# Linear attention and a Swish layer on one core: one batch's early steps a slot later, tangent products in their own chunk, a new order by hand

## The chip, the core and the metric

The kernel runs on one core of a Trainium2 chip. A core has a matrix engine (TensorE, PE in the profile; its weight loads are listed apart as PEld), a vector engine (VectorE, DVE), an engine for activations (ScalarE, ACT), a general engine (GpSimd, POOL) and a queue for transfers (SyncE, SP). The metric is the device time of one execution in microseconds, as the median of several runs.

## What is computed

The reference, cut to what matters. Eight batches of eight heads, 576 positions of 64 numbers; their attention output is the input of a two-layer block with 2048 columns in the middle.

```python
theta = pi / 2 * pos / S
phi(x) = concat(max(x, 0) * cos(theta), max(x, 0) * sin(theta))     # 64 -> 128
kv  = einsum('bhsf,bhsd->bhfd', phi(k), v)
z   = sum(phi(k), over s)
x   = einsum('bhsf,bhfd->bhsd', phi(q), kv) / (phi(q) . z + 1e-6)
# x as (8*576 tokens, 512)
h   = x @ w_in                          # 512 -> 2048
out = (h / (1 + exp(-beta * h))) @ w_out   # 2048 -> 512, float32
```

## The kernel before

The 4608 tokens are worked off in nine chunks of 512. A batch has 576 tokens, nine blocks of 64, so chunk c needs x of batches up to c; the attention of batch c+1 is worked between the matmuls of chunk c.

Attention of one batch: ReLU of q, k (`q_relu`, `k_relu`); v scaled by cosine and by sine (`v_scale`, on DVE or ACT); kv (`kv_mm`, copied out of PSUM by `kv_take`); the queries turned, on TensorE with an identity for batches 0 and 1 (`q_turn_pe`), by a transposing DMA after that (`q_turn_dma`). The cosine of the queries is divided out at the end, so that the second half of the features is the turned query times a table of tangents: the tangent product, `tan_mul`; `q_tan` runs it on GpSimd. `num_mm` multiplies by kv, `x_rden` and `x_mul` divide, and x is turned back (`x_turn_pe` or `x_turn_dma`) into the tile `xt` of its chunk.

The two layers: `h_plain` computes a block of 128 middle columns with four matmuls of 512 columns. `h_fast` does a 2x2 block scheme with seven products instead of eight for four pairs of column blocks (named X, Y, Z, V), and `o_fast` the same for the output of a chunk (x, y for its two halves). The operands of these products are sums and differences: `g_sum` for the middle activations, `x_sum` for x, `wh_sums` and `w_sums` for weights.

Every engine runs its instructions in the order in which the program gives them (`manual_schedule`). This order is written by hand. Three stretches matter here:

*Chunk 0's slots* (the loop at L783). Slots 0 to 15 compute middle columns; slots 16 to 23 multiply the first eight row blocks of `w_out` into the output; slots 24 to 31 one more row block each: slot 24 multiplies by block 8, slot 25 by block 9, up to block 15. Each slot is four matmuls of 512 columns. Before use a row block is cast and scaled by `cast_out(j)`, on DVE (L123) or, with "a", on ACT (L121). After the matmuls of a slot, the entry of the table `early` (L736) of that slot is run. `rest` (slot 4) gives DVE, in this order, casts 0 to 7, the scaling of v, and the ReLUs of k and q of batch 1. `second` is the turn of batch 1's queries with the casts from 8 on.

*Chunks 1 and 2*: a loop of 16 slots (middle columns), then the output products, with batches 2 and 3 between (`h_first` and the code after it). `att_q` does the ReLU and turn of the queries, `v_half` one scaling of v.

*Chunks 3 to 6*: `chunk` walks through the string `ORDER` (L874). p and sp are plain blocks and their activation; X1 to V7 products, and c1X, a2X, SaX and the like their copies, adds and activations; K and kt are kv and its copy; N0 the attention products, x0 to x2 the division and turn of a third of x, each into its own two PSUM banks; s01 to s34 the sums; g0, g1 the tangent products; ox1 to oy7 the output's products; k, q, v, w with a digit prepare the next batches; t the sums of x for the next chunk. When the operations of a set are done, `prep` calls the next load of k, q or v into the freed tile.

Of the kernel before, what the change touches and what calls it, by code (L numbers as in the profile page):

```python
# [17 lines left out]
NQ = 9  # L18
# [4 lines left out]
def kernel(  # L23
# [16 lines left out]
    B, H, S, D = q.shape  # L40
# [76 lines left out]
    def cast_out(j, eng="d"):  # L117
        i, jj = divmod(j, 4)
        st = stages["out", i]
        if eng == "a":  # L120
            nc.scalar.activation(wout[:, j, :], st[:, jj, :], AF.Copy, scale=rbeta[:, j : j + 1])  # L121
        else:
            nc.vector.tensor_scalar(wout[:, j, :], st[:, jj, :],  # L123
                                    scalar1=rbeta[:, j : j + 1], scalar2=None, op0=ALU.mult)
# [141 lines left out]
    def kv_mm(b, jp, bank, jjs=(0, 1)):  # L266
        t = kv_out(jp, bank)
        for n in range(NQ):
            for jj in jjs:
                for g in range(2):  # L270
                    hs = slice(g * HP, (g + 1) * HP)
                    nc.tensor.matmul(  # L272
                        t[jj * HP : (jj + 1) * HP, g], lhsT=rk[hs, n, 2 * jp + jj, :],
                        rhs=vb[hs, n, 2 * jp + jj].rearrange("q s e -> q (s e)"),
                        start=(n == 0), stop=(n == NQ - 1))
# [382 lines left out]
    got = x_rden(2, 0, 0, 7, (0,))  # L658
# [55 lines left out]
    def num_seven(jp, bank):  # L714
        for n in range(7):
            num_mm(1, n, jp, bank, n)
# [3 lines left out]
    def second():  # L720

        takes.append(q_turn_pe(1, 0, 4, hold=True))
        takes.append(q_turn_pe(1, 1, 6, hold=True))
        cast_out(8)
        takes[0]("act", 0)
        takes[0]("dve", 1)
        cast_out(9, "a")
        takes[0]("dve", 0)
        takes[0]("act", 1)
        cast_out(10)  # L730
        for e, i in (("act", 0), ("dve", 1), ("act", 1), ("dve", 0)):
            takes[1](e, i)
        for j in (11, 12, 14, 15):
            cast_out(j, "a")
# [1 line left out]
    early = {  # L736
        4: lambda: (num_mm(0, 8, 0, 2, 0), num_mm(0, 8, 1, 2, 1), rest()),
        15: lambda: v_scale(1, 1, eng="act"),
        22: lambda: (kv_mm(1, 0, 6), kv_mm(1, 1, 6), kv_take((0, 1), 6, "act")),
        23: second,  # L740
        25: lambda: (num_seven(0, 4), x_mul(x_rden(4, 0, 0, 7, (0,)), 0, 7), cast_out(13)),
        26: lambda: (num_seven(1, 6), x_mul(x_rden(6, 0, 0, 7, (1,)), 0, 7)),
        28: lambda: x_turn_pe(1, 0, 7, 4, ("act",), (0,)),
        29: lambda: x_turn_pe(1, 0, 7, 5, ("dve",), (1,)),
    }

    def num_rest():
# [23 lines left out]
        if b + 1 < B:  # L771
            load_raw(b + 1, "k")

    def kv_all(b, bank=6):
        kv_mm(b, 0, bank)
        kv_mm(b, 1, bank)
        kv_take((0, 1), bank)

    def x_part(b, t, bank):
        x_div(t, bank)  # L780
# [30 lines left out]
    for slot in range(16):  # L811
        h_group(1, slot)
        if slot == 0:
            num_rest()
            att_q(2)
            v_half(2, 0)
        if 3 <= slot < NQ:
            v_half(2, 1, slot, slot + 1, "act")
        if slot == 4:
            k_all(2)  # L820
            v_half(2, 1, 0, 3)
        elif slot == 6:
            w_sums()
        elif slot == 11:
            kv_all(2)
            for jp in range(2):
                tan_mul(nc.vector, qs_of(2)[:, jp], qts[0][:, jp], 0, NQ)
    q_relu(3, 0, "act")
# [28 lines left out]
    got = wh_sums(0)  # L857
# [9 lines left out]
    def k_piece(b, j):  # L867
# [4 lines left out]
            load_raw(b + 1, "k")  # L872

    ORDER = (  # L874
        "p0 Y1 X1 c1X p1 X5 c5X sp0 X6 X2 K c1Y X3 cuX kt Y6 X7 p2 a2X a3X Y5 sp1 a7X cuY c5Y Y7 Z1 SaX "
        "X4 c1Z p3 Y3 Y2 SbX sp2 a7Y Z2 s01 Y4 Z5 sp3 Z6 s03 a3Y a2Z p4 SbY V1 a2Y c5Z cuZ Z7 s02 a7Z p5 "
        "SaY c1V V6 Z3 s11 sp4 s12 cuV a3Z V2 Z4 s14 sp5 V5 SbZ c5V V7 p6 a2V V3 SaZ a7V a3V s21 sp6 SaV "
        "p7 s04 s13 V4 s22 SbV s23 sp7 s24 s31 s33 N0 k1 s32 ox1 c1o ox5 k3 c5o k2 ox6 s34 g0 g1 x0 k0 "
        "ox3 oy1 cuo c1y x2 o3x ox2 ox7 v8 oy5 x1 c5y o2x oy6 w8 q0 q1 cuy v2 v6 oy3 o7x v3 w1 oy7 w4 w3 "
        "w7 o7y ox4 v5 t3 w5 oy2 v4 c4x o3y v7 t1 w0 oy4 w6 t2 v1 c4y v0 o2y w2 t4")  # L880
    ORDER_LAST = (
        "E1 c1E E2 F1 X1 a2E c1X c1F X5 X2 E5 X6 c5X E6 cuX c5E cuE X3 a2X Y1 E3 X7 a3X c1Y a3E SaX a7X "
        "E7 SaE F6 Y5 F5 a7E X4 Y2 c5F Y6 SbX F2 F3 a2Y c5Y a2F cuF E4 Z1 Y3 cuY SbE c1Z a3F Y7 F7 a3Y "
# [40 lines left out]
    def chunk(c, b, x, y, parts):  # L924
        steady = {"X": (0, 2, 0, 1), "Y": (4, 3, 4, 5), "Z": (8, 0, 2, 1), "V": (12, 4, 3, 5)}
        end = {"X": (0, 6, 0, 1), "E": (2, 5, 3, 4), "Y": (4, 2, 0, 1), "F": (6, 7, 3, 4), "Z": (8, 6, 0, 1),
               "V": (12, 5, 3, 4)}
        pairs = {n: h_fast(c, at[0], at[1:]) for n, at in (steady if b < B else end).items()}

        def plain_bank(n):  # L930
            return (2 if n == 7 else 6 + n % 2) if b < B else (2, 7)[n % 2]

        plain = [2, 3, 6, 7, 10, 11, 14, 15]
        outs = {"x": x, "y": y}

        def q_next():
            if b + 3 < B:
                load_raw(b + 3, "q")

        def raw_next(name):  # L940
            if b + 2 < B:
                load_raw(b + 2, name)

        xs_all = {"x0", "x1", "x2"}
        take = prep(b, [
            ({"k0", "k1", "k2", "k3"} | xs_all, lambda: raw_next("k")),
            ({"q0", "q1"} | xs_all, q_next),
            ({f"{o}{n}" for o in "vw" for n in range(NQ)}, lambda: raw_next("v"))])
        last_sum = None
        for op in (ORDER if b < B else ORDER_END if c + 1 < NTC else ORDER_LAST).split():  # L950
            n = int(op[-1]) if op[-1].isdigit() else None
            if op == "K":
                kv_mm(b, 0, 4)
                kv_mm(b, 1, 4)
            elif op == "kt":
                kv_take((0, 1), 4)
            elif op[0] == "N":
                for t, bank in enumerate(parts):
                    num_all(b, t, bank)
            elif op[0] == "x":  # L960
                x_part(b, n, parts[n])
                take(op)
            elif op[0] in "kvwq":
                take(op)
            elif op[0] == "t":
                if c + 1 < NTC:
                    x_sum(c + 1, n)
            elif op[0] == "g":
                if b + 1 < B:
                    q_tan(b + 1, n, None if n else last_sum)  # L970
            elif op[0] == "p":
                h_plain(c, plain[n], plain_bank(n), 2 if n < SPLITS.get(c, (0, 0))[0] else 1)
            elif op[:2] == "sp":
                h_silu(c, plain[n], plain_bank(n))
            elif op[0] == "o" and n is not None:
                outs[op[1]][op[2]]()
            elif op[0] == "o":
                outs[op[2]]["a" + op[1]]()
            elif op[0] == "c" and op[2] in "xyo":
                outs["x" if op[2] == "o" else op[2]][op[:2]]()  # L980
            elif op[0] == "s":
                last_sum = g_sum(c, 2 * int(op[1]), 2 * int(op[1]) + 2, n)
            else:
                pair = op[0] if op[0] in pairs else op[-1]
                pairs[pair][op.replace(pair, "")]()
        if b + 2 < B:
            q_turn_dma(b + 2)

    def h_first(c):
        b = c + 1  # L990
        for slot in range(16):
            h_group(c, slot, 2 if slot < SPLITS.get(c, (0, 0))[0] else 1)
            if c == 2:
                if slot == 0:
                    k_all(b)
                    v_half(b, 1, 0, 4)
                if 1 <= slot < 6:
                    v_half(b, 1, slot + 3, slot + 4, "act")
                if slot == 3:
                    att_q(b + 1)  # L1000
                    wh_sums(4)
                if slot == 9:
                    wh_sums(8)
            if slot == (8 if c == 2 else 1):
                kv_all(b)
            if slot in (3, 7, 11):
                g_sums(c, slot // 2 - 1, slot // 2 + 1)
            elif slot in (13, 15):
                sums = g_sums(c, slot // 2, slot // 2 + 1)
        return sums  # L1010

    FAST = 3
    for c in range(2, NTC):
# [4 lines left out]
        if c >= FAST:  # L1018
            chunk(c, b, x, y, parts)
            continue  # L1020
        sums = h_first(c)
        for t, bank in enumerate(parts):
            num_all(b, t, bank)
        q_tan(b + 1, 0, sums)
        q_tan(b + 1, 1)
        for i, n in enumerate("156273"):
            x[n]()
            if n in "156":
# [15 lines left out]
        y["c5"]()  # L1044
        if c == FAST - 1:
            x_sums(c + 1)
            wh_sums(12)
        v_half(b + 1, 1, 2, 3, "act")
        y["6"]()
        y["cu"]()  # L1050
# [5 lines left out]
        y["3"]()  # L1056
        y["a3"]()
        v_half(b + 1, 0, 7, 9)
        v_half(b + 1, 1, 3, 9, "act")
        y["4"]()  # L1060
        y["c4"]()
# [31 lines left out]
```

## Time and profile before

| | |
|---|---|
| time, median of 3 | 278.01 us (277.81 to 278.37) |
| profiled execution, span on the core | 275.6 us |
| busy: PE, PEld, DVE, ACT, POOL | 268.9, 199.8, 221.0, 184.6, 67.8 us |
| granted TensorE clock | 1.00 throughout |
| chain that ended last | PE 83%, DMA 12%, DVE 2% |

The profile's page gives the busy time of each engine, the same in 40 slices, and the chain of work followed back from the last instruction. For single stretches the trace is asked for its timeline: for each engine the start and the length of a run of equal instructions, its line, operation, shapes and count, and in brackets the idle time of the engine before it with what ended it. Times count from the first instruction. A matmul's shown length includes its way through the array, so that neighbours overlap: the distance between starts tells the pace.

### The profile page before, as it was taken

The page shows a single profiled execution, that of the slowest core. Times are in us where ns is not written, and L with a number is a line of the kernel's source. Part 1 is how long each engine was busy: PE and PEld are TensorE (multiplying, and loading weights), DVE is VectorE, ACT ScalarE, POOL GpSimd, SP SyncE. Part 2 cuts the span into 40 slices and gives each one's busy share as a digit, 9 for nine tenths or more (in the row PEclk, how much of TensorE's full clock was granted, in tenths as well). Part 3 has the DMA queues.
Part 4 walks back from the last instruction along what each step waited for, and adds up shares of the span by engine and source line. Part 5 has one row for each costly group of instructions (what it writes and reads, how often), then busy time and mean ns, then how long its engine had stood idle before and what let it go on. Part 6 is the DMA issues. An engine that isn't in the chain of part 4 may idle for free.

```text
span 275.6 us, 9047 instructions
## 1 busy us (share of the span) xinstructions
PE 268.9 (98%) x3749; PEld 199.8 (73%) x3749; DVE 221.0 (80%) x578; ACT 184.6 (67%) x381; POOL 67.8 (25%) x87
## 2 busy tenths in 40 slices
PE   8899999999999999999999999999999999999993
PEld 8554455446875599869866998688768886888683
DVE  5989968599999898599959995899589589558851
ACT  5778757797248657697669756976694289429821
POOL 1444000600087073106420552044300140000000
PEclk9999999999999999999999999999999999999999
DMA  7999999999969999961899199915400640033005
GB/s 248 369 394 382 393 389 312 375 193 377 244 153 309 245 309 295 394 130 38 179 359 267 39 220 301 121 21 107 114 2 12 117 115 2 0 70 86 2 24 130
DMA packets 50745, 54.00 MB, mean 196 GB/s; under 512 B 31232, under 2 KB 31760, under 8 KB 50704
## 3 DMA queue, kind: packets, MB, share of 16 engines
q1 hardware_dynamic: 47744, 45.88, 59.5%
q0 software_dynamic: 2688, 7.34, 8.9%
q8 instruction: 29, 0.48, 0.7%
q10 hardware_dynamic: 272, 0.21, 0.3%
q14 instruction: 12, 0.10, 0.2%
HBM read 36.71 MB, written 9.44 MB: 167 GB/s over the span
## 4 chain that ended last, share of the span: by engine, by line
PE 83%; DMA 12%; DVE 2%; ACT 1%; SPq 1%; issue 0%; ACTq 0%; DVEq 0%
PE ps L547 35%; PE ps L468 16%; PE ps L422 13%; PE ps L380 10%; DMA raw_q<-in_q_dram 7%; DMA w_stage<-in_moe_w_in_dram 5%; PE ps L293 4%; PE ps L517 3%; PE ps L272 2%; DVE win L115 1%; ACT vb L217 1%; SPq L79 1%; PE ps L234 0%; PE ps L352 0%; DVE qb L194 0%
## 5 line engine op out<-in xcount | busy, mean ns | idle before, releaser
L413 ACT ACTIVATE g_t<-ps,beta 128x512 bf16<-128x512 f32 x96 | 61.0, 698 | 3.1 <-DVE ps L498 2.8
L547 PEld LDWEIGHTS <-S 128*128 128x128 bf16 x589 | 51.3, 98 | 5.0
L510 POOL DMA_DIRECT2D out_dram<-o_sb x56 | 33.5, 604 | 66.3 <-ACT o_sb L523 24.6
L380 PE MATMUL ps<-xt,win 128*128 128x512 bf16 (+1 forms) x196 | 42.8, 375 | 0.1
L547 PEld LDWEIGHTS <-g_t 128*128 128x128 bf16 x440 | 38.2, 98 | 4.3 <-issue 0.3
L422 PE MATMUL ps<-xt,win 128*128 128x512 bf16 (+1 forms) x184 | 40.8, 351 | 0.0
L388 ACT ACTIVATE g_t<-ps,beta 128x512 bf16<-128x512 f32 x48 | 32.2, 690 | 8.0 <-PE ps L380 7.8
L380 PEld LDWEIGHTS <-win 128*128 128x128 bf16 x196 | 18.8, 98 | 21.0 <-issue 0.4
L547 PE MATMUL ps<-wout,g_t 128*128 128x256 bf16 (+1 forms) x284 | 31.7, 262 | 0.0
L547 PE MATMUL ps<-wout,S 128*128 128x256 bf16 (+1 forms) x305 | 31.5, 255 | 0.0
L547 PE MATMUL ps<-T,S 128*128 128x256 bf16 (+1 forms) x284 | 30.8, 262 | 0.0
L399 DVE TENSOR_TENSOR S<-g_t 128x512 bf16<-128x512 bf16 (+1 forms) x66 | 25.1, 409 | 3.6 <-ACT g_t L413 2.7
L217 ACT ACTIVATE vb<-raw_v,sin 128x256 bf16<-128x256 f32 (+1 forms) x61 | 27.4, 501 | 0.9 <-DMA raw_v<-in_v_dram 0.9
L222 POOL TENSOR_TENSOR qs<-qt,tanr 128x1152 bf16<-128x1152 bf16 x6 | 14.2, 2382 | 50.8 <-DVE den L304 29.8
L468 PEld LDWEIGHTS <-w_stage 128*128 128x128 bf16 x224 | 21.6, 98 | 6.7
L468 PE MATMUL ps<-w_stage 128*128 128x256 bf16 x168 | 26.2, 272 | 0.0
L422 PEld LDWEIGHTS <-win 128*128 128x128 bf16 x184 | 17.9, 98 | 10.1
L315 DVE TENSOR_TENSOR xs<-ps,rden 128x768 bf16<-128x768 f32 (+4 forms) x26 | 22.8, 883 | 0.8
L219 DVE TENSOR_SCALAR vb<-raw_v,cos 128x256 bf16<-128x256 f32 x63 | 20.5, 380 | 0.1
L468 PEld LDWEIGHTS <-win 128*128 128x128 bf16 x168 | 16.4, 98 | 4.8 <-issue 0.3
L468 PE MATMUL ps<-xt,win 128*128 128x256 bf16 x112 | 19.1, 273 | 0.0
L594 ACT COPY p<-ps 128x256 f32<-128x256 f32 x16 | 6.0, 373 | 17.0 <-PE ps L547 16.9
(105 smaller groups left out, 417.6 us busy)
## 6 DMA issues: line engine op xcount, KB each, us to landing
raw_v<-in_v_dram SPq DMA_DIRECT2D x7, 1152.0 KB, 9.9
raw_k<-in_k_dram SPq DMA_DIRECT2D x7, 1152.0 KB, 7.5
raw_q<-in_q_dram SPq DMA_DIRECT2D x7, 1152.0 KB, 7.7
out_dram<-o_sb POOLq DMA_DIRECT2D x56, 128.0 KB, 4.4
w_stage<-in_moe_w_in_dram SPq DMA_DIRECT2D x3, 1024.0 KB, 13.0
w_stage<-in_moe_w_out_dram SPq DMA_DIRECT2D x2, 1024.0 KB, 8.1
w_stage<-in_moe_w_out_dram SPq DMA_DIRECT2D x4, 512.0 KB, 11.9
out_dram<-o_sb SPq DMA_DIRECT2D x12, 128.0 KB, 2.4
```

Of the source, the lines that this page charges most:

```text
L217: nc.scalar.activation(o, a, AF.Copy, scale=t[:, n : n + 1])
L219: nc.vector.tensor_scalar(o, a, scalar1=t[:, n : n + 1], scalar2=None, op0=ALU.mult)
L222: return eng.tensor_tensor(dst.rearrange("q n (g p) -> q n g p", g=2), src.rearrange("q n (g p) -> q n g p", g=2), tanr[:, n0:n1].unsqueez ...
L315: nc.vector.tensor_tensor(o.rearrange("q j n s d -> q j (n s) d"), nv[:, :, a:z, :, 0:D].rearrange("q j n s d -> q j (n s) d"), rden[:, :, ...
L380: nc.tensor.matmul(ps[:, h_bank(c, jt), i * 64 : (i + w) * 64], lhsT=win[jt // 4][:, mi, (jt % 4) * P : (jt % 4 + 1) * P], rhs=xt[:, i : i ...
L388: nc.scalar.activation(gs[c, jt // 4][:, jt % 4], ps[:, h_bank(c, jt)], AF.Silu, scale=beta[:, jt : jt + 1])
L399: return nc.vector.tensor_tensor(o, l, r, op=op)
L413: nc.scalar.activation(gs[c, jt // 4][:, jt % 4], ps[:, bank], AF.Silu, scale=beta[:, jt : jt + 1])
L422: nc.tensor.matmul(ps[:, bank, o * 64 : z * 64], lhsT=win[jt // 4][:, mi, (jt % 4) * P : (jt % 4 + 1) * P], rhs=xt[:, o:z, jp, g * HP : (g ...
L468: nc.tensor.matmul(dst, lhsT=left[:, g], rhs=right[:, :, g * HP : (g + 1) * HP], start=start and g == 0, stop=stop and g == 1, skip_group_ ...
L510: (eng or own).dma_start(out=out_v[bb, n][:, m0:m1], in_=o_sb[hf * HP : (hf + 1) * HP, m0:m1])
L547: nc.tensor.matmul(dst[:, m : m + w], lhsT=left(i), rhs=right[:, i, m : m + w], start=start and i == 0, stop=stop and i == order[-1], skip ...
```

## The change

It has these parts:

- In chunk 0, kv, the turn of the queries, the attention products and the turn of x of batch 1 all come one slot later, and `cast_out(8)` moves from the turn of the queries (`second`) to the kv entry before it. It is meant to give raw q one slot more to arrive.
- In chunk 1, ACT scales four rows of v (from slot 2) instead of six, DVE five instead of three; kv comes a slot earlier, and ACT instead of DVE copies it.
- The tangent products of batch b run in chunk b-1 itself, early, behind the fifth product's copy of the pair X, instead of in the chunk before, behind the last sum of the activations. That takes them out of DVE's stretch of sums and divisions.
- The turn of the queries of batch b+2 is requested in `q_next`, behind the load of keys, ahead of the load of queries; it was the last request of the chunk.
- The sums of weight column 12 (`wh_sums(12)`) move behind the last DVE scalings of chunk 2.
- `ORDER` is a new string for chunks 3 to 6.

```diff
@@ second()
-        cast_out(8)
         takes[0]("act", 0)
@@ early
-        22: lambda: (kv_mm(1, 0, 6), kv_mm(1, 1, 6), kv_take((0, 1), 6, "act")),
-        23: second,
-        25: lambda: (num_seven(0, 4), x_mul(x_rden(4, 0, 0, 7, (0,)), 0, 7), cast_out(13)),
-        26: lambda: (num_seven(1, 6), x_mul(x_rden(6, 0, 0, 7, (1,)), 0, 7)),
-        28: lambda: x_turn_pe(1, 0, 7, 4, ("act",), (0,)),
-        29: lambda: x_turn_pe(1, 0, 7, 5, ("dve",), (1,)),
+        23: lambda: (kv_mm(1, 0, 6), kv_mm(1, 1, 6), kv_take((0, 1), 6, "act"), cast_out(8)),
+        24: second,
+        26: lambda: (num_seven(0, 4), x_mul(x_rden(4, 0, 0, 7, (0,)), 0, 7), cast_out(13)),
+        27: lambda: (num_seven(1, 6), x_mul(x_rden(6, 0, 0, 7, (1,)), 0, 7)),
+        29: lambda: x_turn_pe(1, 0, 7, 4, ("act",), (0,)),
+        30: lambda: x_turn_pe(1, 0, 7, 5, ("dve",), (1,)),
@@ chunk 1
-        if 3 <= slot < NQ:
-            v_half(2, 1, slot, slot + 1, "act")
+        if 2 <= slot < 6:
+            v_half(2, 1, slot + 3, slot + 4, "act")
         if slot == 4:
             k_all(2)
-            v_half(2, 1, 0, 3)
+            v_half(2, 1, 0, 5)
         elif slot == 6:
             w_sums()
-        elif slot == 11:
-            kv_all(2)
+        elif slot == 10:
+            kv_all(2, eng="act")
@@ ORDER (its beginning; the middle of the new string has g0 g1)
-        "p0 Y1 X1 c1X p1 X5 c5X sp0 X6 X2 K c1Y X3 cuX kt Y6 X7 p2 a2X a3X Y5 sp1 a7X cuY c5Y Y7 Z1 SaX "
+        "Y1 p1 X1 c1Y p0 X2 c1X X6 Y6 X5 cuY a2X K cuX c5X sp0 X7 kt X3 a3X p2 sp1 Y5 SaX Y7 sp2 a7X Y2 X4 Z1 c5Y "
...
@@ chunk()
         def q_next():
+            if b + 2 < B:
+                q_turn_dma(b + 2)
             if b + 3 < B:
                 load_raw(b + 3, "q")
...
             elif op[0] == "g":
-                if b + 1 < B:
-                    q_tan(b + 1, n, None if n else last_sum)
+                if b < B:
+                    q_tan(b, n, None if n else first)
...
-                pairs[pair][op.replace(pair, "")]()
-        if b + 2 < B:
-            q_turn_dma(b + 2)
+                got = pairs[pair][op.replace(pair, "")]()
+                if op == "c5X":
+                    first = got
@@ chunk 2
-        q_tan(b + 1, 0, sums)
-        q_tan(b + 1, 1)
...
         if c == FAST - 1:
             x_sums(c + 1)
-            wh_sums(12)
...
         v_half(b + 1, 0, 7, 9)
+        wh_sums(12)
```

## The prediction

> **What bounds the kernel now.** I read the page first: the engines' shares, and the chain of work that ended last by line.
>
> ```profile
> PE 268.9 (98%) x3749; PEld 199.8 (73%) x3749; DVE 221.0 (80%) x578; ACT 184.6 (67%) x381; POOL 67.8 (25%) x87
> ...
> PE 83%; DMA 12%; DVE 2%; ACT 1%; SPq 1%; issue 0%; ACTq 0%; DVEq 0%
> ```
>
> TensorE is busy nearly always and carries 83% of the chain; the 12% of DMA lies before 40 us. Busy PE time is modelled, so I checked it by the distance between starts. The windows of chunks 3 to 6 (columns: length, PE busy, PEld, DVE, ACT, POOL, clock, DMA share, GB/s) say how evenly they run:
>
> ```profile
> 109.20:137.20 28.00, 28.00 (x433) 23.26 (x431) 22.62 (x63) 20.56 (x44) 9.41 (x10) 1.00 0.68 189
> 137.20:165.35 28.15, 28.15 (x474) 22.58 (x472) 23.39 (x65) 20.96 (x45) 9.52 (x11) 1.00 0.84 225
> 165.35:193.36 28.01, 28.01 (x427) 22.67 (x425) 23.64 (x70) 20.96 (x45) 8.91 (x10) 1.00 0.62 136
> 193.36:221.35 27.99, 27.99 (x419) 21.84 (x417) 20.52 (x56) 15.59 (x33) 4.16 (x9) 1.00 0.30 60
> ```
>
> In the chain, 4 matmuls of 512 columns take 0.87 us and 16 of 256 take 1.75, so 0.217 and 0.109 each. A chunk has 32 of the first (6.9), 56 of the second for its eight fast column blocks (6.1), keys times values (1.15), the attention products (1.4) and 112 of 256 columns for the output (12.3): 27.9 us, plus four changes of tile size at about 0.1 us. That is the whole 28.0. **These four chunks have nothing left to gain from an order.** What an order can still move are the few places where PE stands: near 40 us, and once near 108. The timeline there, per engine (start, length, engine, line, operation, count, and in brackets idle time and its releaser):
>
> ```profile
> 39.01 1.04 PE L517 MATMUL ps<-wout,g_t 128*128 128x512 bf16 x4
> 40.10 1.34 PE L234 MATMUL ps<-ident,qb 128*128 128x128 bf16 x18
> 41.28 1.89 PE L517 MATMUL ps<-wout,g_t 128*128 128x512 bf16 x8
> ...
> 39.28 1.43 DVE L194 TENSOR_SCALAR qb<-raw_q 128x1152 bf16<-128x1152 f32 x2 [1.64 <-DMA raw_q<-in_q_dram]
> 40.64 0.48 DVE L123 TENSOR_SCALAR wout<-w_stage,rbeta 128x512 bf16<-128x512 f32 x1
> 41.04 1.41 DVE L222 TENSOR_TENSOR qs<-ps,tanr 128x512 bf16<-128x512 bf16 x2
> ...
> 40.59 0.69 ACT L239 COPY qt<-ps 128x640 bf16<-128x640 bf16 x1 [0.50 <-PE ps L234]
> 41.18 0.72 ACT L121 ACTIVATE wout<-w_stage,rbeta 128x512 bf16<-128x512 f32 x1
> 41.80 1.17 ACT L239 COPY qt<-ps 128x512 bf16<-128x512 bf16 x2
> ```
>
> Slot 23 is the four matmuls at 39.01; after them the 18 transposes of the queries wait for DVE's two ReLUs, which wait for raw q; then slots 24 and 25. Slot 24 multiplies by row block 8 of `w_out`, which DVE casts at 40.64 to 41.12, behind the ReLUs; slot 25 by block 9, which ACT casts at 41.18 to 41.90, behind its first copy of the turned queries. Both casts finish just before their slot needs them. The transposes fill the wait for cast 8.
>
> **What the Trainium skill says.** (1) "TensorE: Matmul & The Clock Gate", section "Architectural detail: the array is 16× 32×32, not 1× 128×128", has ACT's and DVE's queues as strict FIFO; in "Step-by-step: what each phase is for" the matmuls stay in program order. The trace agrees: DVE, idle 1.64 us, does no cast ahead of the waiting ReLUs. (2) The same page, "What's actually happening": the clock halves after an idle window of about 3.4 us. PE's stalls here are below 0.4 us and every window shows clock 1.00. (3) "SBUF — State Buffer", "Who interferes with whom": GpSimd and DVE share a port pair and block each other. One DVE scaling of v beside a tangent product lasts 0.55 us (at 131.00), four later ones 1.12 together. (4) "TensorEngine Tiling (Array Packing)", "Key Properties": a change of tile size drains the array; I use the trace's 0.1 us.
>
> **The change, part by part.**
>
> *(a) Kv, transposes, attention products and x transposes of batch 1 one slot later; cast 8 before slot 24.* PE's order was: slot 23, transposes, slot 24 (block 8), slot 25 (block 9). It becomes slot 23, kv, slot 24, transposes, slot 25. Block 8 cannot come earlier: its load was issued at 26.57 and takes 14.0 us (the longest of the line's DMA landings), so 40.6; and the cast stands behind the ReLUs, which end at 40.71. Nothing here touches those loads. So, by the durations above:
> - slot 22 ends at 37.8, slot 23 at 38.7, kv (1.15 from 37.86 to 39.01) at 39.9. Slot 24 could start, but waits for cast 8 (41.12 plus 0.07, as from ReLU's end at 40.03 to the transposes at 40.10): 41.19. **Idle 1.3 us.** Slot 24 ends at 42.06.
> - Transposes: 18 at 0.053 = 0.96 us, to 43.0. ACT's copy starts 0.49 after their start (40.10 to 40.59) and its cast ends 1.80 after it (40.10 to 41.90): 43.86. Slot 25 needs that cast: 43.9 instead of 43.0. **Idle 0.9 us.**
> - Slot 26, 44.8: DVE takes two queries' parts from about 42.8 (1.3 us) and casts block 10 by 44.6. No wait. The attention products of the first half start at 45.75 and the next slot could at 46.33 (0.58, as 43.10 to 43.68). ACT: the third and fourth copies end at 45.7, cast 11 at 46.46, so slot 27 starts at 46.5: **idle 0.2 us.** Casts 12 to 15 follow every 0.62 us and are ahead of their slots (0.87 each).
> - Gone are the transposes' waits of today: slot 23 ended at 39.88, so 0.22 to 40.10, and a second of 0.16 before the second half (first start 40.10, next slot at 41.28: 1.18 against 0.96). **0.4 us saved.**
>
> Sum: 1.3 + 0.9 + 0.2 - 0.4 = **2.0 us later** when chunk 1 begins (50.34 today, 52.3 then; the x copies end at 52.3, but the second half of x is needed only 0.43 later). Can it be regained? From 50 us PE is saturated, so the delay runs to the end.
>
> *(b) Chunk 1: DVE scales five rows of v instead of three, ACT four instead of six; kv one slot earlier and its copy on ACT instead of DVE.* DVE: 2 x 0.27 more, 0.69 less, before the tangent products that end at 66.71, 1.0 before PE's 67.73. ACT: 2 x 0.52 less, 0.6 more, and it waits 7.8 us in all for PE at L388. No cost: hidden beside matmuls.
>
> *(c) The sums of weight column 12 behind the last DVE scalings of chunk 2.* Today four of them (106.43 to 107.44) stand before the two adds that PE's last product waits for: its matmul before starts at 107.79, the next at 108.16, where 0.1 would do. Without the sums the add can follow its product at about 107.2 and end at 107.6, before PE wants it. **0.3 us saved.** What waits behind the sums in turn are chunk 3's first DVE adds, which PE reaches some 2 us after its start; hidden.
>
> *(d) Tangent products at the head of their own chunk.* Ten in all before and after, 2.38 us each on POOL, 25% busy. They start behind a copy some 3 us into the chunk and need 4.8 us, so end at about 8 us; PE reads the result at 14.3 us (123.5 less 109.2). Port contention moves from DVE's scalings to a stretch of adds on PSUM. Zero.
>
> *(e) Turn of queries behind the load of keys.* The turn's reader is the next chunk, its source the ReLUs of the same chunk; it landed 12 us after its request (110.04 to 121.98) with time to spare. Earlier is not needed. Zero.
>
> *(f) The new order.* I added up both orders with the rows' durations (ACT Silu 0.57 between starts, DVE add 0.34, sum 0.34, division 1.4 per part, matmuls as above), each engine in its order and each PSUM bank free before its next use. The old order came out without PE waits beyond 0.02 us and with its last DVE sum 0.2 us from the traced one; the new one has a PE wait below 0.1 us a chunk, though thin: the second output product enters bank 0 some 0.3 us after its division left it. Bounds 0 and 0.3 us a chunk; I take zero.
>
> **Sum:** 278.0 + 2.0 - 0.3 = **279.7 us.**
>
> **Rivals.**
> - *The shift only takes waits away*: the transposes no longer wait for q and nothing takes that wait's place; with (c), 278.0 - 0.4 - 0.3 = 277.3. For it: 0.4 us of PE waits do stand there. Against: cast 8, in DVE's order, ends after slot 24 is due, by 1.3 us. Chance 0.07.
> - *Regained*: waits in chunk 1 or 2 swallow the delay, ending near 278.0. Against: their matmuls stand edge to edge. Chance 0.04.
> - *The new order also stalls*, 0.3 us a chunk in four chunks: 279.7 + 1.2 = 280.9. For it: the thin bank distance. Chance 0.12.
> - *The clock drops*: PE would work only about 1.8 of 4.1 us (39.9 to 43.9). If one window of 3.4 us ran at half speed, some 1.7 to 3.4 more: about 282. Against: no single idle piece exceeds 1.3 us. Chance 0.04.
> - The forecast keeps 0.73.
>
> **The numbers.** Of the forecast, the two waits are fixed by landings and in-order queues within perhaps 0.4 us each; 279.0 to 280.5 covers it, and reaching up to the stalling order gives 278.9 to 281.0. Left out are the first two rivals, the clock, and a little of each tail. Chances: faster 0.08, within 0.2% (0.56 us) 0.05, slower 0.87.
>
> **What would show it.** In the changed profile: slot 24's matmuls at about 41.2 with PE idle before them, released by DVE's cast; slot 25 at about 43.9, released by ACT's cast; chunk 1's first matmul near 52.3; no gap at the end of chunk 2; chunks 3 to 6 at 28.0 to 28.1 us each; POOL's tangent products in their first third. The forecast is wrong if DVE casts block 8 before its ReLUs, if raw q or block 8 lands earlier, or if a chunk's length moves by more than 0.1 us.

## The result, and the profile after

| | before | changed |
|---|---|---|
| time, median | 278.12 us (4 runs) | 282.88 us (281.38 to 287.21, 4 runs) |
| the same change run again on another occasion | 278.17 us | 282.11 us (281.66 to 282.45, 4 runs) |
| ratio to before | | 1.0154, 95% interval 1.011 to 1.0197; again 1.0141, 1.0114 to 1.0168 |
| span in the profile | 275.6 us | 280.8 us |

The change is slower by 1.4 to 1.5%; forecast were 279.7 us and at most 281.0. Ratios, here and below, leave out disturbed executions (over 1.5% above a kernel's fastest); medians and ranges hold them.

The page of the changed kernel: the engines' shares, the granted clock in 40 slices, the chain by engine.

```profile
PE 270.0 (96%) x3745; PEld 200.9 (72%) x3749; DVE 221.7 (79%) x579; ACT 184.8 (66%) x380; POOL 67.1 (24%) x87
...
PEclk9999997999999999999999999999999999999999
...
PE 82%; DMA 11%; DVE 3%; ACT 1%; issue 1%; SPq 1%; ACTq 0%; DVEq 0%
```

Matmul work is unchanged, its share fell from 98 to 96%: TensorE stands more. The clock has a dip near 42 to 49 us that the kernel before did not have, and "issue", waiting for nothing that the profile shows, now has 1% of the chain. The view of waits, for TensorE alone (us in total, times, longest), names two new ones at its top:

```profile
PE ps L517 <- DVE wout L123: 2.0, 1, 2.0
PE ps L293 <- issue: 1.6, 3, 0.7
```

The first is slot 24's wait for cast 8. The second lies in the attention products (L293), once each in chunks 1, 4 and 5. The timeline around slot 24, TensorE, then DVE, then ACT:

```profile
38.48 1.22 PE L272 MATMUL ps<-vb,rk 64*64 64x130 bf16 x72
41.69 1.15 PE L517 MATMUL ps<-wout,g_t 128*128 128x512 bf16 x3 [1.99 <-DVE wout L123]
42.63 2.13 PE L234 MATMUL ps<-ident,qb 128*128 128x128 bf16 x18
44.77 2.41 PE L517 MATMUL ps<-wout,g_t 128*128 128x512 bf16 x8
...
39.79 1.43 DVE L194 TENSOR_SCALAR qb<-raw_q 128x1152 bf16<-128x1152 f32 x2 [1.64 <-DMA raw_q<-in_q_dram]
41.15 0.49 DVE L123 TENSOR_SCALAR wout<-w_stage,rbeta 128x512 bf16<-128x512 f32 x1
...
44.00 0.73 ACT L121 ACTIVATE wout<-w_stage,rbeta 128x512 bf16<-128x512 f32 x1
```

Kv, then idle, then slot 24 as cast 8 ends at 41.64. Raw q came 0.5 us later in this execution than in the one profiled before. Then the 18 transposes need 2.14 us from first to next start instead of the forecast's 0.96, and slot 25 follows as cast 9 ends at 44.73: the windows 40 to 44 and 44 to 48 (columns as before) show the clock at 0.81 and 0.77.

```profile
40.00:44.00 4.00, 2.26 (x16) 1.75 (x17) 1.73 (x4) 1.19 (x3) 0.00 (x0) 0.81 1.23 300
44.00:48.00 4.00, 3.98 (x73) 2.11 (x72) 3.23 (x6) 3.46 (x7) 0.00 (x0) 0.77 0.85 292
```

Cut more finely, the clock is at 0.51 from 42.5 to 45.9 us and full before and after: half speed for 3.4 us. Chunk 1 begins at 53.48 us in this profile, 3.1 us later than before (50.34).

The second profile of the same kernel has the wait without the dip, and so the second wait too, for cast 9 on ACT. Its TensorE timeline:

```profile
41.70 1.02 PE L517 MATMUL ps<-wout,g_t 128*128 128x512 bf16 x3 [1.58 <-DVE wout L123]
42.56 1.17 PE L234 MATMUL ps<-ident,qb 128*128 128x128 bf16 x18
44.40 1.89 PE L517 MATMUL ps<-wout,g_t 128*128 128x512 bf16 x8 [0.68 <-ACT wout L121]
```

The rest comes later. The windows of chunks 3 to 5, changed kernel (cut so that the attention products lie 14 to 16 us inside each):

```profile
113.10:141.20 28.10, 28.10 (x433) 23.31 (x432) 23.41 (x66) 20.81 (x47) 8.06 (x9) 1.00 0.63 175
141.20:169.90 28.70, 28.24 (x474) 22.60 (x472) 23.75 (x65) 20.83 (x47) 9.00 (x11) 1.00 0.99 211
169.90:198.80 28.90, 28.23 (x427) 22.74 (x426) 24.05 (x71) 20.85 (x47) 8.97 (x11) 1.00 0.67 149
```

Chunk 3 has its 28.1 us; chunks 4 and 5 have 28.7 and 28.9, with 0.46 and 0.67 us in which no matmul ran. Both stand in the middle of the attention products; in chunk 4, TensorE's timeline:

```profile
155.81 0.19 PE L293 MATMUL ps<-kv,qs 64*64 64x65 bf16 x1
156.46 0.22 PE L293 MATMUL ps<-kv,qs 64*64 64x65 bf16 x3 [0.46 <-issue]
```

Neither matmul waits for a semaphore. What is short there is instructions. They come over transfer queues of their own; the list of queues has one of 29 packets of 16 KB, which I call pages:

```profile
q8 instruction: 29, 0.48, 0.7%
```

That it is TensorE's fits its 3745 matmuls and 3749 weight loads, some 260 instructions to a page. The page that these products need started its transfer at 153.9, 1.1 us before the products, and landed at 154.9; in the kernel before it started at 147.8, 3.7 us before them. Three things in the traces tie the stands in chunks 3 to 5 to these pages. In the changed kernel and in experiments 1, 5, 8 and 12 TensorE stops at the same matmul of a chunk, behind the 93rd recorded one of the 144 products in chunk 4 and the 124th in chunk 5. In experiment 3, which adds eight matmuls ahead of them, it stops eight earlier, behind the 85th and the 116th. And it goes on 1.2 to 1.5 us after the page has landed, every time.

How much slack a page has differs by chunk. In the kernel before, some 4.5 us pass in chunk 4 from the start of the page's transfer to the matmul that needs it, but 2.8 us in chunk 5, where the page starts only nine matmuls ahead of the tiny products. Transfer (1.65 and 1.2 us) and the 1.2 to 1.5 us after it take 2.9 to 3.2 and 2.4 to 2.7: chunk 5 has almost nothing to spare.

The stand in chunk 1 (0.44 us at 72 us) and one of 0.55 us in chunk 2 in the second profile end in the same way, some 1.5 us after a page landed. Experiment 7 has one of 0.5 us in chunk 2 as well, where its kernel is still that of before. No experiment takes apart why those pages were late.

### The profile page after: what moved, and what is told of

It is laid out like the page before. It is cut to its first block, busy times and chain, and to the rows that moved or that the text cites. A ratio compares the mean times of both kernels' runs of the same rounds, so it can differ in the third digit from the quotient of the medians.

```text
span 280.8 us, 9050 instructions
## 1 busy us (share of the span) xinstructions
PE 270.0 (96%) x3745; PEld 200.9 (72%) x3749; DVE 221.7 (79%) x579; ACT 184.8 (66%) x380; POOL 67.1 (24%) x87
## 4 chain that ended last, share of the span: by engine, by line
PE 82%; DMA 11%; DVE 3%; ACT 1%; issue 1%; SPq 1%; ACTq 0%; DVEq 0%
PE ps L547 34%; PE ps L468 16%; PE ps L422 12%; PE ps L380 10%; DMA raw_q<-in_q_dram 8%; PE ps L293 4%; DMA raw_k<-in_k_dram 3%; PE ps L517 3%; PE ps L272 2%; ACT qb L192 1%; DVE xs L315 1%; PE ps L234 1%; DVE qb L194 1%; SPq L79 1%; PE ps L352 0%
## 5 line engine op out<-in xcount | busy, mean ns | idle before, releaser
L510 POOL DMA_DIRECT2D out_dram<-o_sb x56 | 32.7, 590 | 121.8 <-DVE o_sb L597 75.2
L547 PE MATMUL ps<-wout,S 128*128 128x256 bf16 (+1 forms) x305 | 32.1, 255 | 0.0
L547 PE MATMUL ps<-T,S 128*128 128x256 bf16 (+1 forms) x284 | 31.4, 262 | 0.2 <-ACT p L593 0.2
L217 ACT ACTIVATE vb<-raw_v,sin 128x256 bf16<-128x256 f32 (+1 forms) x59 | 25.9, 500 | 1.5 <-DMA raw_v<-in_v_dram 1.5
L468 PE MATMUL ps<-w_stage 128*128 128x256 bf16 x168 | 26.9, 273 | 0.0
L468 PE MATMUL ps<-xt,win 128*128 128x256 bf16 x112 | 20.4, 272 | 0.0
L219 DVE TENSOR_SCALAR vb<-raw_v,cos 128x256 bf16<-128x256 f32 x63 | 18.7, 361 | 0.5 <-DMA raw_v<-in_v_dram 0.5
L496 DVE TENSOR_TENSOR ps<-ps,p 128x256 f32<-128x256 f32 x28 | 11.9, 429 | 7.4 <-PE ps L468 5.9
```

The source lines that it names most:

```text
L217: nc.scalar.activation(o, a, AF.Copy, scale=t[:, n : n + 1])
L219: nc.vector.tensor_scalar(o, a, scalar1=t[:, n : n + 1], scalar2=None, op0=ALU.mult)
L468: nc.tensor.matmul(dst, lhsT=left[:, g], rhs=right[:, :, g * HP : (g + 1) * HP], start=start and g == 0, stop=stop and g == 1, skip_group_ ...
L510: (eng or own).dma_start(out=out_v[bb, n][:, m0:m1], in_=o_sb[hf * HP : (hf + 1) * HP, m0:m1])
L547: nc.tensor.matmul(dst[:, m : m + w], lhsT=left(i), rhs=right[:, i, m : m + w], start=start and i == 0, stop=stop and i == order[-1], skip ...
```

## The experiments

Each was built from the kernel before or the changed one. First, four together that split the change.

**1. All but the early shift.**

```diff
 (the changed kernel)
-        23: lambda: (kv_mm(1, 0, 6), kv_mm(1, 1, 6), kv_take((0, 1), 6, "act"), cast_out(8)),
-        24: second,
...
+        22: lambda: (kv_mm(1, 0, 6), kv_mm(1, 1, 6), kv_take((0, 1), 6, "act")),
+        23: second,
...
```

> The change with batch 1's early steps put back to their old slots, cast 8 back in the turn of the queries; all else as changed. Theory (three costs: the wait of slot 24, the clock that drops after it, and waits for instruction pages inside the attention products): the first two go, the third stays: 279.2 us, with TensorE waits of 0.5 to 0.9 us inside the attention products of chunks 4 and 5. Rival 'all of it is the early shift': 277.8 us. Rival 'the early shift costs only its 2.0 us wait': 281.

Measured: 279.73 us (14 runs), ratio 1.006 (1.0037 to 1.0083). The clock stays at 1.00 from 40 to 48 us. Its waits of TensorE keep the second of the two:

```profile
PE ps L293 <- issue: 1.1, 2, 0.6
```

So the rest of the change costs about 1.6 us, which leaves 2.4 to 3.2 for the early shift.

**2. Only the early shift.**

```diff
 (the kernel before)
-        22: lambda: (kv_mm(1, 0, 6), kv_mm(1, 1, 6), kv_take((0, 1), 6, "act")),
-        23: second,
...
+        23: lambda: (kv_mm(1, 0, 6), kv_mm(1, 1, 6), kv_take((0, 1), 6, "act"), cast_out(8)),
+        24: second,
...
```

> The kernel before with the early shift alone. Theory: wait of slot 24 of about 2 us, clock below 0.85 from 40 to 48 us, then chunks 3 to 6 at 28.0 us each: 281.3 us. Rival 'only the 2.0 us wait, clock kept': 280.1 us. Rival 'the early shift costs nothing by itself': 278.1 us.

Measured: 280.27 us (5 runs), ratio 1.0076 (1.0038 to 1.0115): 2.1 us, the rival without a clock drop. Its TensorE timeline has all three waits of the prediction, and slots 24, 25 and 27 start at 41.23, 43.93 and 46.57 us (forecast 41.19, 43.9 and 46.5):

```profile
41.23 1.02 PE L517 MATMUL ps<-wout,g_t 128*128 128x512 bf16 x3 [0.75 <-DVE wout L123]
42.09 1.17 PE L234 MATMUL ps<-ident,qb 128*128 128x128 bf16 x18
43.93 1.89 PE L517 MATMUL ps<-wout,g_t 128*128 128x512 bf16 x8 [0.67 <-ACT wout L121]
46.57 0.38 PE L517 MATMUL ps<-wout,g_t 128*128 128x512 bf16 x1 [0.17 <-ACT wout L121]
```

Chunk 1 begins at 52.35 us; 52.3 was forecast. Experiments 1 and 2 add up: 278.1 + 1.6 + 2.1 = 281.8 us against 282.1 and 282.9 measured.

**3. The wait filled with matmuls on a constant.**

```diff
 (the changed kernel)
-        23: lambda: (kv_mm(1, 0, 6), kv_mm(1, 1, 6), kv_take((0, 1), 6, "act"), cast_out(8)),
+        23: lambda: (kv_mm(1, 0, 6), kv_mm(1, 1, 6), warm_pe(8, bank=4), kv_take((0, 1), 6, "act"), cast_out(8)),
```

> The change with eight matmuls of 512 columns on a constant, into a PSUM bank that is free then, between kv and slot 24 (1.7 us of added work that fits in the wait of slot 24). Theory that the clock drops because TensorE stood: clock 1.00 from 40 to 48 us, the transposes take 0.96 us again, slot 25 now waits for cast 9, and chunk 1 begins some 0.8 us earlier than in the change: 282.0 against 282.9 us. Rival 'the clock drop has another cause, or the added work itself delays': no gain, 282.9 us or more.

Measured: 282.06 us (4 runs), ratio 1.014 (1.0097 to 1.0183); not told apart from the changed kernel. In its profile the clock is 1.00 from 40 to 48 us and slot 25 waits 0.68 us for cast 9, as the theory has it; but as the drop is not in every execution, the median says nothing on it. The same profile shows a drop elsewhere: after a stand of 1.8 us in the attention products of chunk 5 its clock has a mean of 0.57 over four microseconds (half speed for 3.4 us).

**4. The early shift undone, and the turn of queries back at the end of the chunk.**

```diff
 (the kernel of experiment 1)
         def q_next():
-            if b + 2 < B:
-                q_turn_dma(b + 2)
...
                 if op == "c5X":
                     first = got
+        if b + 2 < B:
+            q_turn_dma(b + 2)
```

> As the first kernel, and the turn of the queries requested at the end of the chunk again, as before the change; new order, tangent products in their own chunk and the moved sums stay. Theory: the loads of q and v are no longer held up behind the turn, the instruction pages come in time, and the attention products of chunks 4 and 5 run without waits: 277.8 us. Rival 'the new order itself stalls': 279.2 us, as the first kernel.

Measured: 277.95 us (20 runs), ratio 0.9989 (0.9971 to 1.0006). With the turn back, the 1.6 us are gone. Four more runs ask why; the last of them is the changed kernel again (its numbers are above).

> The changed kernel once more, for more executions and a second profile. Theory that the clock drops after the wait of slot 24 only in part of the executions, since the kernel before with the early shift alone kept it: mean clocks between 0.99 and 1.00, those below 0.997 some 1 to 2 us slower than those at 1.000; median 282.5 us. Rival 'the drop belongs to every execution of this kernel': all clocks at 0.994 or less.

All four clocks were 0.997 or more, so the drop is in part of the executions; 282.11 us without it is close to the 282.58 us of the execution at 0.994 on the first occasion, beside which stood 281.38 and 283.19 at about 1.0.

**5. The turn behind the load of q.**

```diff
 (the kernel of experiment 1)
-            if b + 2 < B:
-                q_turn_dma(b + 2)
             if b + 3 < B:
                 load_raw(b + 3, "q")
+            if b + 2 < B:
+                q_turn_dma(b + 2)
```

> The change with batch 1's early steps back in their old slots, and in chunks 3 to 5 the turn of the queries requested behind the load of queries instead of ahead of it (still ahead of the load of v, still in mid-chunk). Theory that the turn's slow issue on the transfer queue pushes the loads of q and v into the attention products of the next chunk: q lands some 8 us earlier, v is still late; between 277.9 and 279.7, about 278.8 us. Rival 'the turn itself, wherever it stands in mid-chunk, makes the instruction pages late': 279.7 us, as with the turn ahead.

Measured: 278.82 us (20 runs), ratio 1.0015 (0.9994 to 1.0036): between the two, as expected, though the interval does not tell it from the kernel before. In its profile chunk 4's products run through, chunk 5's stand for 1.0 us. That fits: chunk 4 loads no q (only eight batches exist), so there the order of requests is that of experiment 1.

**6. Without the loads that come late.**

```diff
 (the kernel of experiment 1)
-                load_raw(b + 3, "q")
+                raws["q", b + 3] = raws["q", b + 2]
...
-            if b + 2 < B:
+            if b + 2 < B and name == "v":
+                raws["v", b + 2] = raws["v", b + 1]
+            elif b + 2 < B:
                 load_raw(b + 2, name)
```

> The change with batch 1's early steps back in their old slots, and without the loads of q for batch 7 and of v for batches 6 and 7 in chunks 3 and 4 (the tiles of the batches before are used again, so the output of these batches is not the reference's). The turn stays in mid-chunk. Theory that loads running into the attention products make the instruction pages late: no waits above 0.2 us inside the attention products of chunks 4 and 5, 277.9 us. Rival 'the turn alone or the new order makes them': 279.7 us, waits of 0.6 us as before.

Measured: 277.47 us (20 runs), ratio 0.9976 (0.9963 to 0.999). No wait in chunks 4 and 5. The turn stays in mid-chunk and the cost is gone: it is carried by the loads. One wait of 0.6 us stands in chunk 3, ahead of which nothing was taken out; its page started at 121.8, when the last load (v) had landed at 120.4 and the turn of queries was still under way (to 123.1).

**7. Only the turn's new place, with the old order.**

```diff
 (the kernel before)
         def q_next():
+            if b + 2 < B:
+                q_turn_dma(b + 2)
             if b + 3 < B:
...
-        if b + 2 < B:
-            q_turn_dma(b + 2)
```

> The kernel before with one part of the change: the turn of the queries requested ahead of the load of queries in chunks 3 and 4 instead of at their end. Theory (the turn's place alone makes the late pages): waits of 0.5 to 0.9 us inside the attention products of chunks 4 and 5, 279.6 us. Rival 'it needs the new order or the tangent products' new place': 278.1 us.

Measured: 278.08 us (12 runs), ratio 1.001 (0.9989 to 1.003). The theory as I had put it fails: the place of the turn alone costs nothing that shows. It needs something else of the change.

**8. More traffic in the kernel before.**

```diff
 (the kernel before)
         if b + 2 < B:
             q_turn_dma(b + 2)
+            load_raw(b + 2, "v")
```

> The kernel before, order and turn untouched, with one more load of the same v (1.2 MB) behind the turn at the end of chunks 3 and 4, which runs into the attention products of the next chunk. Theory that loads which run there make instruction pages late: waits of 0.5 to 1.5 us inside the attention products of chunks 4 and 5 with nothing else changed, 279.5 us. Rival 'the late pages come from the new order or the turn's place and not from traffic': 278.1 us.

Measured: 281.62 us (20 runs, 277.6 to 283.47), ratio 1.0062 (1.0032 to 1.0091), so 1.7 us by the ratio. Order and turn are untouched, and a long "issue" wait stands in chunk 5's attention products:

```profile
PE ps L293 <- issue: 1.9, 1, 1.9
```

with the clock at 0.62 in the four microseconds that follow it (windows):

```profile
181.00:184.00 3.00, 1.15 (x94) 0.97 (x82) 2.90 (x10) 1.36 (x3) 0.39 (x1) 0.94 0.63 245
184.00:188.00 4.00, 4.00 (x24) 2.97 (x24) 1.98 (x4) 1.57 (x4) 4.00 (x2) 0.62 0.29 61
```

The page that these products need took 2.7 us from the start of its transfer, against 1.2 in the kernel before. Twelve of the twenty executions have a mean clock of 0.994 or less, all at 281.59 us or more; the other eight, at 0.996 or more, have 280.99 or less. The median of these eight, 279.3 us, is still 1.4 above the kernel before: the added load costs time without a drop of the clock too.

**9. What the new order adds: the old order with the tangent products moved.**

```diff
 (the kernel of experiment 1 with the old string for chunks 3 to 6; what differs from the old string)
-        "SaY c1V V6 Z3 s11 sp4 s12 cuV a3Z V2 Z4 s14 sp5 V5 SbZ c5V V7 p6 a2V V3 SaZ a7V a3V s21 sp6 SaV "
-        "p7 s04 s13 V4 s22 SbV s23 sp7 s24 s31 s33 N0 k1 s32 ox1 c1o ox5 k3 c5o k2 ox6 s34 g0 g1 x0 k0 "
+        "SaY c1V g0 g1 V6 Z3 s11 sp4 s12 cuV a3Z V2 Z4 s14 sp5 V5 SbZ c5V V7 p6 a2V V3 SaZ a7V a3V s21 sp6 SaV "
+        "p7 s04 s13 V4 s22 SbV s23 sp7 s24 s31 s33 N0 k1 s32 ox1 c1o ox5 k3 c5o k2 ox6 s34 x0 k0 "
```

> The change with batch 1's early steps in their old slots and with the old order of chunks 3 to 6, in which only the tangent products are moved to their own chunk (behind the first copy of the pair V). Turn in mid-chunk as in the change. Open is what makes the mid-chunk turn cost 1.6 us with the new order and tangent products and nothing with the old ones. Theory A, the tangent products' place (they no longer hold back stores on their engine): 279.7 us, with waits in the attention products of chunks 4 and 5. Theory B, the rest of the new order (it uses the bandwidth later in the chunk): 278.1 us, without them.

Measured: 277.91 us (12 runs), ratio 0.9991 (0.9959 to 1.0024), no wait in any attention product of its profile. Theory B: mid-chunk turn and early tangent products cost nothing that shows with the old order; with the new one the turn costs 1.6 us.

The lists of transfers from 158 to 186 us (KB each, us from request to landing) show the difference; first experiment 1, then experiment 9:

```profile
raw_v<-in_v_dram SPq DMA_DIRECT2D x1, 1152.0 KB, 11.4
...
qt<-qb SPq DMA_TRANSPOSE x1, 15.2
```

```profile
raw_v<-in_v_dram SPq DMA_DIRECT2D x1, 1152.0 KB, 9.6
...
qt<-qb SPq DMA_TRANSPOSE x1, 13.0
```

And the transfer queue's timeline there, in the same order:

```profile
162.56 0.52 SPq L79 DMA_DIRECT2D raw_k<-in_k_dram  x1
163.17 7.35 SPq L252 DMA_TRANSPOSE qt<-qb  x1
170.69 0.88 SPq L79 DMA_DIRECT2D raw_v<-in_v_dram  x1
```

```profile
160.57 0.52 SPq L79 DMA_DIRECT2D raw_k<-in_k_dram  x1
161.20 6.42 SPq L252 DMA_TRANSPOSE qt<-qb  x1
167.79 0.53 SPq L79 DMA_DIRECT2D raw_v<-in_v_dram  x1
```

The request of one turn holds the queue for 6.4 to 7.4 us, and what is requested behind it starts that much later. The new order divides and turns the last third of x later, so that keys are requested 2 us later, then comes the turn; v lands at 170.69 + 11.4 = 182.1, inside chunk 5's products (180.7 to 182.8), instead of 177.4, before them (179.1). Most of its bytes move just ahead of the products, when the page should come (windows, experiment 1, then experiment 9):

```profile
175.00:180.00 5.00, 5.00 (x34) 3.15 (x33) 4.77 (x14) 4.48 (x10) 0.00 (x0) 1.00 0.83 283
180.00:182.00 2.00, 1.99 (x129) 1.41 (x127) 1.81 (x6) 2.00 (x5) 0.00 (x0) 1.00 0.18 55
```

```profile
175.00:180.00 5.00, 5.00 (x132) 3.38 (x132) 4.63 (x14) 4.85 (x10) 0.00 (x0) 1.00 0.13 45
180.00:182.00 2.00, 2.00 (x72) 1.80 (x63) 1.97 (x7) 1.50 (x4) 0.00 (x0) 1.00 0.04 8
```

In experiment 1 the page starts at 180.0, as the load's traffic ends; in experiment 9 at 177.4, well after it. So in this chunk it is the traffic ahead of the products that counts, rather than that in them. The table has, from the trace, how long before the first of the attention products their page started, and the longest distance of two starts in these products where it is 0.15 us or more:

| kernel | chunk 4: page ahead by, longest stand | chunk 5: page ahead by, longest stand |
|---|---|---|
| before | 3.7 us, - | 1.7 us, - |
| changed | 1.1 us, 0.65 us | 0.4 us, 0.86 us |
| changed, again | 2.2 us, - | 0.2 us, 1.20 us |
| 1: all but the early shift | 1.1 us, 0.70 us | 0.6 us, 0.74 us |
| 3: wait filled | 1.7 us, 0.50 us | 0.5 us behind, 1.94 us |
| 4: turn back as well | 3.4 us, - | 1.7 us, - |
| 5: turn behind q | 3.8 us, - | 0.1 us, 1.20 us |
| 6: without the late loads | 4.0 us, - | 1.2 us, - |
| 7: turn alone | 3.6 us, - | 1.0 us, 0.19 us |
| 8: more traffic | 4.2 us, - | 1.0 us (in transfer for 2.7), 2.04 us |
| 9: old order, tangent products moved | 1.9 us, - | 1.6 us, - |
| 12, second profile | 4.1 us, - | 0.3 us, 0.96 us |

In chunk 4 of experiment 9 the loads of q and v run into the products as well (products from 150.9 to 152.2, landings at 152.0 and 154.9), and the page starts only 1.9 us ahead; it comes in time by some tenths of a microsecond, and not because the loads were kept out. Nor must it be a load, or the change, that makes a page late: in the second profile of experiment 12 (old order, turn at the end of the chunk) the page of chunk 5 starts at 180.9, when the last load had landed at 178.7 and the turn was under way (to 183.1). The same holds for a stand of 1.7 us in chunk 3 of experiment 4. The kernel before ranges from 277.1 to 280.2 us beside experiments 1 to 4; whether late pages make that spread was not looked at.

**10. The moved sums alone.**

```diff
 (the kernel before)
             x_sums(c + 1)
-            wh_sums(12)
...
         v_half(b + 1, 0, 7, 9)
+        wh_sums(12)
```

> The kernel before with one part of the change: the sums of weight column 12 behind the last scalings of chunk 2. Prediction's term (c): 0.3 us saved, 277.8 us, and the distance between the two matmul starts at the end of chunk 2 falls from 0.36 to about 0.1 us. Rival: another wait takes its place, 278.1 us.

Measured: 278.07 us (22 runs), before 277.95; ratio 0.9982 (0.9964 to 1.0001); not told apart. The trace has the gain, in TensorE's timeline, before and then alone:

```profile
106.07 1.95 PE L547 MATMUL ps<-wout,S 128*128 128x256 bf16 x30
108.16 1.05 PE L547 MATMUL ps<-T,g_t 128*128 128x256 bf16 x15
```

```profile
106.22 1.94 PE L547 MATMUL ps<-wout,S 128*128 128x256 bf16 x30
108.00 1.05 PE L547 MATMUL ps<-T,g_t 128*128 128x256 bf16 x15
```

2.09 us from first to next start became 1.78: 0.3 us, which the spread of executions hides in the median.

**11. The sums and chunk 1's part.**

```diff
 (the kernel of experiment 10)
...
-        if 3 <= slot < NQ:
-            v_half(2, 1, slot, slot + 1, "act")
+        if 2 <= slot < 6:
+            v_half(2, 1, slot + 3, slot + 4, "act")
...
-        elif slot == 11:
-            kv_all(2)
+        elif slot == 10:
+            kv_all(2, eng="act")
```

> The kernel before with the moved sums and chunk 1's part of the change (scalings, kv a slot earlier, copy on ACT), and with the old order, tangent products and turn. Chunk 1's part is forecast at nothing: 277.8 us. Rival 'chunk 1's part costs or gains': beyond 0.3 us from the kernel with the sums alone.

Measured: 278.06 us (22 runs), ratio 0.9996 (0.9978 to 1.0015), against 278.07 with the sums alone: chunk 1's part costs and brings nothing.

**12. The shift with the transposes ahead of slot 24**, run twice.

```diff
 (the kernel of experiment 2)
-        23: lambda: (kv_mm(1, 0, 6), kv_mm(1, 1, 6), kv_take((0, 1), 6, "act"), cast_out(8)),
-        24: second,
+        23: lambda: (kv_mm(1, 0, 6), kv_mm(1, 1, 6), kv_take((0, 1), 6, "act"), second()),
...
```

(cast 8 stands at the beginning of `second` again, as before the change)

> The kernel before with the early shift, but with the turn of batch 1's queries (and cast 8 in it) kept ahead of slot 24; kv, attention products and x transposes one slot later as in the change. Theory that slot 24 placed ahead of the transposes is the whole cost of the shift, since the transposes no longer fill the wait for cast 8 and cast 9 stands behind them: 278.1 us, no idle before slot 24 or 25. Rival 'the later kv or attention products cost it': 280.2 us.

> The early shift with the turn ahead of slot 24 once more, for a second profile: the first run's median was 279.05 us, while its profiled execution, at 277.43, showed no wait more than the kernel before. Theory 'the shift itself leaves a small cost that varies between executions, from an instruction page or the late landing of q': a median near 279 us again and, in a profile above 278.5 us, one wait of 0.5 us or more that the kernel before does not have. Rival 'chance of that chip': 278.1 us.

Measured: 279.05 and 279.03 us (20 runs each), ratios 1.0039 (1.0014 to 1.0063) and 1.0036 (1.0018 to 1.0054). Neither theory holds alone: 1.0 to 1.3 us of the shift's 2.1 vanish with slot 24's waits, 0.8 to 1.1 stay. The second profile shows part of it, a wait that this variant itself makes: the second half of the transposes writes into the PSUM bank that kv has just left and waits for ACT's copy of it.

```profile
40.32 0.68 PE L234 MATMUL ps<-ident,qb 128*128 128x128 bf16 x9
41.46 0.66 PE L234 MATMUL ps<-ident,qb 128*128 128x128 bf16 x9 [0.46 <-ACT kv L282]
```

It has, besides, waits for instructions in the attention products at 46 and 182 us (1.1 us in all); the first profile has none of these waits. Whether kv's later place costs anything where slot 24 comes first is left open.

## Why the prediction was wrong

- *Bound.* Right: TensorE sets the time, and from the attention products of chunk 3 on to those of chunk 6 no order brought a chunk below 28.0 us. What it missed is that a chunk has one more supply beside operands and banks: its instructions.
- *(a) 2.0 us for the early shift.* Right in mechanism and size: 2.1 us alone, with the starts of the slots within 0.1 us of the forecast (experiment 2). The waits 1.3, 0.9 and 0.2 came out as 1.58 and 0.68 (changed kernel, second profile) and as 0.75, 0.67 and 0.17 (experiment 2). The first depends on how far TensorE was when q landed, and that differs from one execution to the next. That the starts were met so closely is partly luck: raw q's landing alone moved by 0.5 us between two profiles. Experiment 12 does not bear out that slot 24's place is the whole of it.
- *(b) chunk 1, zero.* Right (experiment 11).
- *(c) 0.3 us saved.* Right in the trace, not resolved in the medians.
- *(d) tangent products, zero.* Right (experiment 9).
- ***(e) and (f), the failed step.*** "Earlier is not needed. Zero." looked at who reads the turned queries. It did not ask who stands behind the turn's request on the transfer queue, though the trace of before showed that request holding the queue for 9 to 11 us (110.04, 138.55). "I take zero" for the new order looked at engines and banks. Neither shows a cost alone (experiments 4 and 7); together they push the loads up to and into the attention products, and the instruction pages for these come late: 1.6 us instead of zero (experiments 1, 4, 5, 6, 8). The prediction had itself named a chunk's length moving by more than 0.1 us as a sign of being wrong: chunks 4 and 5 came out at 28.7 and 28.9 us. That loads in flight make pages late is shown by adding and removing them; how pages and data share the transfer engines was not tried.
- *The rest of the gap.* From 279.7 to 282.1 us are 2.4. All but the shift was put at 0.3 us saved and cost 1.6: that is 1.9. The shift adds 0.1, the kernel before 0.2 (278.17 for 278.0); 0.2 are not accounted for.
- *The rival "the new order also stalls"*, 280.9 us, had the right stretch and near the right sum (1.2 us), but named the wrong wait. The distance to bank 0 cost nothing that shows.
- *The rival "the clock drops"*, chance 0.04, happens, but in part of the executions. "The Trainium skill", page "TensorE: Matmul & The Clock Gate", section "What's actually happening", gives an idle window of about 3.4 us; I took an idle piece of 1.3 us for safe; in the first profile it was 1.99. Here the clock fell after idle pieces of 1.99 us (changed kernel), 1.85 (experiment 8) and 1.8 (experiment 3), each time to half for 3.4 us; after 1.58 and 0.68 (second profile) and 1.53 (experiment 4) it did not. So no piece had to be as long as the window. The page calls the window free-running, which would fit a drop in some executions only. It is not needed for the changed kernel's median: 282.11 us came without it.
- *The range.* 281.0 as upper end held the shift and a stall of 1.2 us in the new order together. It left no room for the 1.6 us that order and turn cost, nor for (c) saving nothing.

Experiments 4, 9, 10 and 11 lie within 0.2% of the kernel before; none was shown to be faster.

## What to carry to other kernels

When a step is moved ahead of a wait, list what used to fill that wait and which in-order casts stand behind the moved step: here the transposes had filled it, and moving them made two casts late. When a transfer's request is moved, cost it by what is requested behind it and by where these loads will then run, not only by its own reader. Where TensorE issues hundreds of tiny matmuls in little more than a microsecond, keep large transfers out of that stretch and out of the two to four microseconds ahead of it: its instruction pages can come late.

## What the hardware showed that I had not expected

- Instructions are a stream that can run dry: a page of 16 KB takes 0.9 to 2.7 us in transfer in these profiles (0.9 to 1.65 in that of the kernel before), and TensorE goes on 1.2 to 1.5 us after it has landed, while the attention products use up about a page (144 matmuls, each with a weight load) in 1.3 us. "The Trainium skill", page "Runtime: NRT & Kernel Launch", section "Instruction fetch mechanics", has blocks of 16 KiB, 256 instructions, whose crossing is "mostly hidden"; here it cost up to 1.9 us at one place (experiment 8).
- One request of a transposing transfer occupies its queue for 4.3 to 11.5 us in the profile before, so that every load behind it starts that much later.
- A stand of 1.8 to 2 us can be followed by 3.4 us at half the clock. In experiment 8 that separates the executions at 281.6 us and more from those at 281.0 and less.
